# Order of work in a windowed-attention kernel: K's second part in its own bank, odd heads' outer products first, statistics moved behind one transpose

## The chip, the cores and the metric

The kernel runs on one core of one Trainium2 chip. The metric is device time in microseconds (us) for one execution of the whole program.

## What is computed

One block of a conditioned mixer, all in bf16. x has 2048 rows of 512 features. Attention has 32 heads of 16 features and a causal window of 256 rows; a token mixer follows, an MLP over the 2048 rows with 1792 hidden units.

```python
mod = (silu(c) @ w_mod).reshape(1, 6, 1, 512)             # sa, ca, ga, sb, cb, gb
h = layernorm(x) * (1 + ca) + sa
q, k, v = split(h @ wqkv)                                 # 32 heads of 16
p = softmax(where(0 <= i - j < 256, q @ k.T / 4, -1e9))
x = x + ga * ((p @ v) @ wo)
h = layernorm(layernorm(x) * (1 + cb) + sb)
u = gelu(einsum('sd,sf->df', h, w1) + b1)
x = x + gb * (u @ w2 + b2).T
```

## The kernel before

**Stages.** Four groups of rows (tg, 512 rows each) go through attention one after the other. Each has four groups of heads (g8, eight heads each), and each of these has five units k: two units of scores for the even heads (kind A), one for the masked corners of even and odd heads together (kind C, k = 2), and two for the odd heads (kind A). In tg 0 the first two A units are merged for g8 > 0, so that there are 77 units in all. After attention comes the MLP, mostly one long row of matmuls.

**A unit.** `emit_scores` (line 595) lets TensorE write the scores of eight heads into two PSUM tiles `pss` (a ring of three tiles of two banks). `emit_exp` (662) is ScalarE's exponential of each of the two, two a unit. `av_a` (680) multiplies the exponentials of an A unit with V, `av_c` (696) those of the C unit; both add into one PSUM bank, `po`, of which there is only one. I call these the outer products; the even heads' close after k = 2, the odd heads' after k = 4. Then `norm_out` (732) transposes the bank on VectorE (line 735), which frees it, and `norm_rest` (740) divides by the sums (VectorE line 746, GpSimd 747) and transposes back (755). In `av_a` the first matmul of the even or odd heads opens the bank (`start`), and the last of `av_c` closes it (`stop`).

**Other work of the same stretch.** TensorE also computes the projections of Q, K and V, the output projection and the first MLP products, one "group" of 16 matmuls a unit, into the single bank `dn`; VectorE evacuates each (lines 304, 330, 333, 397, 838), and only then can the next group start. VectorE and GpSimd also run the layer norms: `ln1_stats` (225) and `ln1_apply` (250, on GpSimd for tg > 0), `ln23` (758; line 775 is its normalisation) whose results `hb` the groups of `part_group` (822) read.

**The order** is written out by the loop from line 989 on. For each unit it issues the first exponential, the scores of the next unit, outer products that close a bank, the group's matmuls, the second exponential, the group's evacuation, and then the outer products of the unit before. Within that, VectorE's remaining work stands in chains of steps. A planner places them: `clock` holds an estimate of when each engine is free, `fill(until)` (805) issues steps as long as their estimated cost ends before `until` plus a slack (`SLACK`, and `late[0]`), and a step may carry a condition. `products` (960) calls `fill` ahead of each transpose that closes a bank. So a changed cost in the planner moves VectorE's and GpSimd's instructions for the rest of attention.

**The head.** For the first unit Q and K are computed in two parts (`first_qk`, 551): Q's first 320 columns go to a `dn` bank, K's first 128 to a `po` bank, and both second parts to the two banks of one tile, `second` (547), which is one of the three `pss` tiles. VectorE masks Q into even and odd heads (`q_half`, 559), ScalarE copies K (`k_piece`, 567). The first scores need only the first parts; the second unit's scores need the rest, and write the bank pair that `second` held. `modulate` (530) makes the rows that both read, in two column parts, feature blocks 0 and 1 on VectorE, 2 and 3 on ScalarE.

Of the kernel before, what the change touches and what calls it, by code (L numbers as in the profile page):

```python
# [8 lines left out]
DT = mybir.dt  # L9
# [3 lines left out]
P = 128  # L13
S = 2048
D = 512
# [5 lines left out]
ND = D // P  # L21
# [9 lines left out]
def kernel(  # L31
# [67 lines left out]
    part = {fc: ppool.tile([P, D], DT.float32, name=f"part{fc}") for fc in PART}  # L99
# [123 lines left out]
    ln1 = {}  # L223
# [60 lines left out]
    def dense(out, lhsT, rhs, start, stop):  # L284

        for j in range(4):
            cols = slice(32 * j, 32 * j + 32)
            nc.tensor.matmul(  # L288
                out[cols, :], lhsT=lhsT[:, cols], rhs=rhs, start=start, stop=stop,
                tile_position=(0, 32 * j), skip_group_check=True,  # L290
            )
# [123 lines left out]
    with tc.manual_schedule():  # L415
# [130 lines left out]

        second = ps_s.tile([P, 2, 4 * P], DT.float32, name="pss")
        pq2 = (ps_dn.tile([P, 4 * P], DT.float32, name="dn"), second[:, 0, :])
        pk2 = (ps_po.tile([P, 4 * P], DT.float32, name="po"), second[:, 1, :])

        def first_qk(dc, part):
            q_cols, k_cols = ((slice(0, FIRST), slice(0, P)), (slice(FIRST, 4 * P), slice(P, 4 * P)))[part]
            for ps, col0, cols in ((pq2[part], 0, q_cols), (pk2[part], D, k_cols)):
                dense(
                    ps[:, cols], lhsT=wqkv[:, dc, col0 : col0 + P], rhs=h1T[0][:, dc, cols],
                    start=(dc == 0), stop=(dc == ND - 1),
                )

        def q_half(part):
            cols = (slice(0, FIRST), slice(FIRST, 4 * P))[part]  # L560
# [8 lines left out]
            nc.scalar.activation(out=KT[0][0][:, cols], in_=pk2[part][:, cols], func=ACT.Copy)  # L569

        for dc in (0, 2, 1, 3):
            first_qk(dc, 0)
        q_half(0)
        k_piece(0)
        for dc in (0, 2):
            first_qk(dc, 1)

        w1box = {}

# [9 lines left out]
        def a_pieces(tg, i):  # L589
            return [(4 * tg + kb, q0, n, c0) for kb, q0, n, c0 in A_PIECES[i] if 4 * tg + kb >= 0]  # L590
# [71 lines left out]
        def emit_exp(u, a):  # L662
# [14 lines left out]
            )  # L677
            return act.ins

        def av_a(tg, g8, k):  # L680
            kind, par, i = KINDS[k]
            if i == 0:
                state["po"] = ps_po.tile([P, 4 * P], DT.float32, name="po")
            merged = i == 0 and both(tg, g8, 0)
            k, shift = (0, 256 * par) if merged else (k, 0)
            for n, (kb, q0, nq, c0) in enumerate(a_pieces(tg, i)):
                c0 += shift
                for j in range(4):
                    nc.tensor.matmul(  # L689
                        state["po"][32 * j : 32 * j + 32, q0 : q0 + nq],  # L690
                        lhsT=VaugT[kb // 4][:, kb % 4, 8 * g8 + 2 * j + par, :],
                        rhs=state["e", tg, g8, k, j // 2][:, j % 2, c0 : c0 + nq],
                        start=(i == 0 and n == 0), stop=False, tile_position=(0, 32 * j), skip_group_check=True,
                    )

        def av_c(tg, g8, par):
            for b in range(4):
                for half in range(2):
                    if half and 4 * tg + b < 2:
                        continue  # L700
                    c0, q0 = 256 * par + 64 * b, b * P + 64 * half
                    for j in range(4):
                        nc.tensor.matmul(  # L703
                            state["po"][32 * j : 32 * j + 32, q0 : q0 + 64],
                            lhsT=Vc[half][:, b, 8 * g8 + 2 * j + par, :],
                            rhs=state["e", tg, g8, 2, j // 2][:, j % 2, c0 : c0 + 64],
                            start=False, stop=(b, half) == (3, 1), tile_position=(0, 32 * j),
                            skip_group_check=True,
                        )

        def copy_vc(g8, half, b, n, kb):
# [11 lines left out]
        def emit_av(u):  # L723
            tg, g8, k = units[u]
            if k != 2:
                av_a(tg, g8, k)
            if k in (2, 4):
                av_c(tg, g8, k // 4)
                norm_out(k // 4)
                return True  # L730

# [172 lines left out]
        def at_unit(tg, ul, u, behind):  # L904
            if ul == 0 and tg + 1 < NG:
                st = lambda g, t0=0: [
                    (lambda tl=tl: ln1_stats(g, tl), 0.8, lambda tl=tl: 4 * g + tl in loaded) for tl in range(t0, 4)
                ]

                def ap(*tls):  # L910
                    for tl in tls:
                        ln1_apply(tg + 1, tl)
                    return 1.13 * len(tls)
                if tg == 0:
                    steps = st(1, 2)
                    steps[1] = (lambda: (ln1_stats(1, 3), on_pool(ap(2, 3)))[0], *steps[1][1:])
                else:
                    steps = [(lambda tl=tl: ap(tl), 0.0) for tl in range(4)]
                add_chain(steps, first=True)
                if tg == 0:  # L920
                    add_chain(st(2) + st(3))
            if tg == 0 and ul == 8:
                zeros_for(3)
                on_pool(1.9)
            if tg == 0 and ul == 3:
                nc.gpsimd.memset(mod_add[:], 0.0)
                nc.gpsimd.memset(mod_add[32:64, :], 1.0)
                nc.gpsimd.tensor_copy(out=sT_rep[:], in_=sT[:].unsqueeze(2).to_broadcast([P, ND, 32]))
                on_pool(0.9)
            if tg == 0 and 7 <= ul < 11:  # L930
                loaded.update((2 * ul - 6, 2 * ul - 5))
            for n in ((0, 1, 2, 3), (4, 5))[ul] if tg == 0 and ul < 2 else ():
                late_mod(n, behind)
            for g8 in range(ND):
                if ul == ((0, 3, 7, 10) if tg == 0 else (0, 3, 4, 5))[g8] and (g8 or tg < 2):
                    copies_for(tg, g8)
            for n in (6, 7) if tg == 0 and ul == 2 else ():
                late_mod(n, behind)
            if 0 < tg < NG - 1 and ul == 17:
                copies_for(tg + 1, 0)  # L940
            while q_loads and ul != 3:
                load_q(*q_loads.pop(0))
            if tg == 0 and 4 <= ul < 8:
                pair = slice(2 * ul, 2 * ul + 2)
                paced(xall[:, pair, :], x_rows[:, pair, :], behind)
            if tg == 0 and 8 <= ul < 10:
                js = slice(ul % 2 * 2, ul % 2 * 2 + 2)
                paced(wod[:, js, :], wo_v[:, js, :], behind)
            if tg == 1 and ul == 2:
                modw.release()  # L950
                w1box["pool"] = tc.alloc_tile_pool(name="w1pool", bufs=1, side="right")
                w1box["a"] = w1box["pool"].tile([P, NA, F], DT.bfloat16, name="w1a")
                w1box["v"] = B_w1.rearrange("(sc p) f -> p sc f", p=P)
                w1box["sc"] = iter([(sc, n) for sc in range(NA) for n in range(2)])

            for sc, n in [x for x in [next(w1box.get("sc", iter(())), None)] if x]:
                part_f = slice(n * F // 2, (n + 1) * F // 2)
                paced(w1box["a"][:, sc, part_f], w1box["v"][:, sc, part_f], behind)

        def products(u):  # L960
            tg, g8, k = units[u]
            if k in (0, 3):
                clock["pe"] = max(clock["pe"], clock["po"])
            clock["pe"] += (0.34, 0.34, 0.25, 0.34, 0.58)[k]
            if k in (2, 4):
                fill(clock["pe"])
                clock["dve"] = max(clock["dve"], clock["pe"] + 0.05) + 0.73
                clock["po"] = clock["dve"] + 0.1
            if emit_av(u) and k == 4:
                add_chain(norm_rest(tg, g8), first=True)  # L970
# [7 lines left out]
                on_pool(for_pool)  # L978

        emit_scores(0)  # L980
        for dc in (1, 3):
            first_qk(dc, 1)
        q_half(1)
        v0_mms, v0_evac, _ = v_group(0, 0, ps_dn)
        v0_evac(v0_mms())
# [3 lines left out]
        for u, (tg, g8, k) in enumerate(units):  # L989
# [9 lines left out]
            if u + 1 < len(units):  # L999
                emit_scores(u + 1)  # L1000
                if units[u + 1][2] == 2:
                    first = max(clock["pe"], before) + 0.3
                    clock["pe"] = max(first, clock["act"] + 0.05) + 0.42
                else:
                    first = clock["pe"] = max(clock["pe"], clock["act"] - 0.1) + 0.4
                ready[u + 1] = (first + 0.1, clock["pe"] + 0.1)
            for n in range(3) if u == 4 else ():
                products(n)
            closes = u > 0 and units[u - 1][2] in (2, 4) and u != 3
# [9 lines left out]
            group = at.get(ul)  # L1019
            held[0] = u < 4  # L1020

            late[0] = 0.5 if 4 <= u < 8 else 0.0
            if group:
                tile_ = group[0]()
                clock["pe"] = max(clock["pe"], clock["dn"]) + (0.55 if group[2] > 1 else 0.2 if group[2] == 0.2 else 0.9)
# [227 lines left out]
```

## Time and profile before

| what | us |
|---|---|
| median of 3 runs | 258.14 |
| the runs | 257.07 to 258.76 |
| profiled execution | 256.86 |
| its span on the core | 255.2 |
| TensorE, ScalarE, VectorE, GpSimd busy | 237.4, 160.8, 170.2, 132.8 |
| first exponential | 12.41 |
| end of the last exponential | 161.96 |

The profile names engines PE (TensorE matmul), PEld (its weight loads), DVE (VectorE), ACT (ScalarE), POOL (GpSimd) and SP (the queue that issues DMAs). A timeline row gives start, duration, engine, line and operation, output and inputs by the program's names, and in brackets how long the engine had been idle and what is taken to have released it. Consecutive instructions of one kind are merged into one row; since matmuls are pipelined, a row's end lies after the start of the next. The time of an execution is its span and some 1.7 us around it.

### The profile page before, as it was taken

To read this page: it belongs to the slowest core of one execution; us is meant where nothing else is said; L and a number is where in the kernel's file an instruction comes from. 1 tells how busy PE (TensorE), PEld (TensorE's weight loads), DVE (VectorE), ACT (ScalarE), POOL (GpSimd) and SP (SyncE) were. 2 spreads that over 40 slices of the span, in tenths; PEclk is the share of its full clock that TensorE was granted. 3 is DMA by queue.
4 is the path that set the end of the run, shared out by engine and by line. 5 is a ranking of instruction groups with operands and counts; after the bars stand their busy time and mean duration, and the time that the engine had idled before them with its cause. 6 is when DMAs were issued, how large, how long until landed. Compare 5 with 4: busy or idle time off the path is not lost.

```text
span 255.2 us, 11303 instructions
## 1 busy us (share of the span) xinstructions
PE 237.4 (93%) x5011; PEld 127.1 (50%) x5011; DVE 170.2 (67%) x358; ACT 160.8 (63%) x187; POOL 132.8 (52%) x225
## 2 busy tenths in 40 slices
PE   7989879989989999989999999999999999999994
PEld 2534445555555556555555555544444444444443
DVE  5768789795898868988877895689512303342544
ACT  6478999999999999999999999300074220000000
POOL 5696875986368998977726798654200000000000
PEclk9999999999999999999999999999999999999999
DMA  6986715146620714201123200799960000202121
GB/s 174 317 274 198 210 57 157 37 105 145 208 78 21 219 34 85 46 17 24 41 46 68 60 3 6 260 411 410 410 240 0 0 0 3 82 7 75 39 86 41
DMA packets 26260, 29.96 MB, mean 117 GB/s; under 512 B 3940, under 2 KB 22884, under 8 KB 26212
## 3 DMA queue, kind: packets, MB, share of 16 engines
q1 hardware_dynamic: 26212, 29.25, 36.8%
q8 instruction: 39, 0.64, 1.1%
q14 instruction: 9, 0.07, 0.1%
HBM read 22.55 MB, written 2.23 MB: 97 GB/s over the span
## 4 chain that ended last, share of the span: by engine, by line
PE 67%; DVE 24%; DMA 3%; issue 2%; SPq 2%; POOL 1%; ACT 0%; DVEq 0%
PE py L1216 19%; PE dn L288 18%; PE pu L1094 8%; PE pu L1180 6%; DVE t L735 4%; PE pss L608 3%; DVE VaugT L304 3%; PE po L689 3%; PE po L703 3%; DVE KT L330 2%; DVE qs L333 2%; DVE ln_stats L229 2%; DVE x L397 2%; DVE ln_stats L763 1%; PE pa L1116 1%
## 5 line engine op out<-in xcount | busy, mean ns | idle before, releaser
L675 ACT ACTIVATE et<-pss 128x1024 bf16<-128x1024 f32 (+1 forms) x154 | 144.2, 1016 | 4.6 <-PE pss L625 3.2
L1216 PE MATMUL py<-guT,w2r 128*128 128x512 bf16 (+1 forms) x238 | 48.5, 366 | 0.0
L1216 PEld LDWEIGHTS <-w2r 128*128 128x128 bf16 x238 | 23.3, 98 | 25.3
L288 PE MATMUL dn<-h1T,wqkv 128*32 128x512 bf16 (+1 forms) x480 | 31.4, 378 | 3.2 <-DVE qs L333 1.3
L1195 DVE SCALAR_TENSOR_TENSOR o<-py,bFM,bc 128x512 bf16<-128x512 f32 (+1 forms) x17 | 11.7, 716 | 30.5 <-PE py L1216 30.5
L735 DVE STREAM_TRANSPOSE t<-po 128x512 f32<-128x512 f32 x32 | 22.6, 707 | 7.7 <-PE po L703 7.4
L212 POOL TENSOR_TENSOR ln_rstd<-ln_ve,mhalf 128x1 f32<-128x1 f32 (+1 forms) x40 | 24.1, 603 | 3.6 <-DVE ln_ve L208 0.4
L689 PE MATMUL po<-et,VaugT 128*32 128x64 bf16 (+2 forms) x704 | 24.8, 240 | 1.1 <-DVE t L735 1.1
L608 PE MATMUL pss<-QT,KT 32*128 32x64 bf16 (+2 forms) x704 | 24.7, 237 | 0.7 <-ACT KT L569 0.6
L689 PEld LDWEIGHTS <-VaugT 128*32 128x32 bf16 x704 | 18.1, 96 | 12.3 <-issue 4.4
L208 POOL TENSOR_SCALAR ln_ve<-ln_mv 128x1 f32<-128x1 f32 (+1 forms) x39 | 9.1, 234 | 25.1 <-DVE ln_mv L765 13.5
L288 PEld LDWEIGHTS <-wqkv 128*32 128x32 bf16 x544 | 13.7, 95 | 13.0 <-issue 5.5
L608 PEld LDWEIGHTS <-KT 32*128 32x128 bf16 x704 | 13.5, 92 | 13.2 <-issue 4.4
L747 POOL TENSOR_TENSOR merge<-t,zr 128x512 bf16<-128x512 f32 x16 | 16.9, 1058 | 3.6 <-DVE zr L746 3.6
L1105 ACT ACT_TABLE_LOAD x1 | 1.3, 1283 | 24.7 <-DMA w2r<-in_B_w_dram 24.7
L288 PE MATMUL dn<-wqkv,h1T 128*32 128x512 bf16 x224 | 14.7, 380 | 2.2 <-DVE qs L333 0.9
L779 POOL TENSOR_TENSOR h<-h,bc 128x512 bf16<-128x512 bf16 x12 | 13.9, 1160 | 4.7 <-DVE h L775 4.7
L625 PE MATMUL pss<-mask_q,mask_k 32*128 32x256 bf16 (+1 forms) x232 | 16.3, 266 | 0.0
L1103 DVE TENSOR_TENSOR gelu_a<-pu,part 128x512 f32<-128x512 f32 x8 | 5.2, 686 | 16.4 <-PE pu L1180 16.4
L780 POOL TENSOR_TENSOR h<-h,bc 128x512 bf16<-128x512 bf16 x12 | 13.9, 1161 | 0.9
L288 PE MATMUL dn<-wod,OTd 128*32 128x512 bf16 x192 | 12.6, 380 | 1.9 <-DVE part L838 0.7
L1180 PE MATMUL pu<-hb,w1b 128*128 128x512 bf16 x64 | 14.3, 379 | 0.0
(126 smaller groups left out, 377.7 us busy)
## 6 DMA issues: line engine op xcount, KB each, us to landing
w2r<-in_B_w_dram SPq DMA_DIRECT2D x14, 512.0 KB, 10.0
w1a<-in_B_w_dram SPq DMA_DIRECT2D x16, 224.0 KB, 3.7
w1b<-in_B_w_dram SPq DMA_DIRECT2D x8, 448.0 KB, 7.3
wmod<-in_w_mod_dram SPq DMA_DIRECT2D x8, 256.0 KB, 4.3
Vc<-VaugT SPq DMA_DIRECT2D x32, 64.0 KB, 2.8
out_dram<-otile SPq DMA_DIRECT2D x15, 128.0 KB, 1.7
x<-in_A_x_dram SPq DMA_DIRECT2D x7, 256.0 KB, 4.6
Vc<-VaugT SPq DMA_DIRECT2D x12, 128.0 KB, 3.3
```

Source lines behind the costliest of these rows:

```text
L212: nc.gpsimd.tensor_tensor(out=r[:], in0=ve[:], in1=mhalf[:, 0:n], op=ALU.pow)
L288: nc.tensor.matmul(out[cols, :], lhsT=lhsT[:, cols], rhs=rhs, start=start, stop=stop, tile_position=(0, 32 * j), skip_group_check=True,)
L608: nc.tensor.matmul(pss[j // 2][:, j % 2, c0 : c0 + nq], lhsT=keys(kb, g8)[rows[j], k0 : k0 + P], rhs=QT[tg][g8][rows[j], p, q0 : q0 + nq], ...
L625: nc.tensor.matmul(pss[j // 2][:, j % 2, :].rearrange("p (a r) -> p a r", a=2)[:, 0:n, :] .rearrange("p a (b q) -> p a b q", q=64)[:, :, 0 ...
L675: act = nc.scalar.activation(out=et[:, :, 0:n], in_=state.pop((u, a))[:, :, 0:n], func=ACT.Exp, scale=SCORE_SCALE,)
L689: nc.tensor.matmul(state["po"][32 * j : 32 * j + 32, q0 : q0 + nq], lhsT=VaugT[kb // 4][:, kb % 4, 8 * g8 + 2 * j + par, :], rhs=state["e" ...
L735: nc.vector.transpose(out=state["t2"][:, par, :], in_=state["po"][:])
L747: nc.gpsimd.tensor_tensor(out=m[:].rearrange("p (b a d) -> p a b d", a=2, d=DH), in0=t2v[:, :, :, 0:DH], in1=zr[:].to_broadcast([P, 2, 16, ...
L779: nc.gpsimd.tensor_tensor(out=h2[:], in0=h2[:], in1=bc_cb1, op=ALU.mult)
L1094: nc.tensor.matmul(pu[:, i, :], lhsT=w1_of(sc, fc), rhs=hb[sc][:], start=(sc == 0), stop=(sc == NT - 1),)
L1180: nc.tensor.matmul(pu[:, i, :], lhsT=w1_of(sc, fc), rhs=hb[sc][:], start=(sc == s0), stop=(sc == NT - 1),)
L1216: nc.tensor.matmul(pys[n][:, 0 : hi - lo], lhsT=w2r[:, fc, tb * P : (tb + 1) * P], rhs=guT[fc][:, lo:hi], start=(fc == 0), stop=(fc == NF ...
```

## The change

Five edits, with no arithmetic added or left out.

1. Head: K's second part goes to the `po` bank and its first part to the second bank of `second`, beside Q's second part. All of K's second part is computed ahead of the first scores, all of Q's behind them (before, half of each ahead and half behind).
2. For tg > 0 the odd heads' `av_c` opens the bank instead of closing it. It is issued in the iteration of k = 4, right behind the next unit's scores and ahead of that iteration's group; `av_a` of k = 3 then adds, and that of k = 4 closes. The planner's cost of closing the odd heads falls from 0.58 to 0.34, and its slack for tg > 0 rises by 0.12.
3. `av_c` takes its blocks in the order 0, 1, 3, 2.
4. `fill` is not called ahead of the transpose of unit 7, so that no statistics are placed there.
5. A step of `ln1_apply` waits in the planner until its statistics have been placed.

```diff
-        pk2 = (ps_po.tile([P, 4 * P], DT.float32, name="po"), second[:, 1, :])
+        pk2 = (second[:, 1, :], ps_po.tile([P, 4 * P], DT.float32, name="po"))
...
         for dc in (0, 2, 1, 3):
-            first_qk(dc, 0)
+            first_qk("q", dc, 0)
+            first_qk("k", dc, 0)
         q_half(0)
         k_piece(0)
-        for dc in (0, 2):
-            first_qk(dc, 1)
+        for dc in range(ND):
+            first_qk("k", dc, 1)
...
+        def outer_first(tg, par):
+
+            return tg > 0 and par == 1
+
         def av_a(tg, g8, k):
             kind, par, i = KINDS[k]
-            if i == 0:
+            opened = outer_first(tg, par)
+            if i == 0 and not opened:
                 state["po"] = ps_po.tile([P, 4 * P], DT.float32, name="po")
...
-                        start=(i == 0 and n == 0), stop=False, tile_position=(0, 32 * j), skip_group_check=True,
+                        start=(i == 0 and n == 0 and not opened),
+                        stop=(opened and i == 1 and n == len(pieces) - 1),
+                        tile_position=(0, 32 * j), skip_group_check=True,
...
         def av_c(tg, g8, par):
-            for b in range(4):
+            opens = outer_first(tg, par)
+            if opens:
+                state["po"] = ps_po.tile([P, 4 * P], DT.float32, name="po")
+            for b in (0, 1, 3, 2):
...
-                            start=False, stop=(b, half) == (3, 1), tile_position=(0, 32 * j),
-                            skip_group_check=True,
+                            start=(opens and (b, half) == (0, 0)), stop=(not opens and (b, half) == (2, 1)),
+                            tile_position=(0, 32 * j), skip_group_check=True,
...
             if k in (2, 4):
-                av_c(tg, g8, k // 4)
+                if not outer_first(tg, k // 4):
+                    av_c(tg, g8, k // 4)
                 norm_out(k // 4)
...
-                    steps = [(lambda tl=tl: ap(tl), 0.0) for tl in range(4)]
+                    steps = [(lambda tl=tl: ap(tl), 0.0, lambda tl=tl: (tg + 1, tl // 2) in ln1) for tl in range(4)]
...
-            clock["pe"] += (0.34, 0.34, 0.25, 0.34, 0.58)[k]
+            clock["pe"] += (0.34, 0.34, 0.25, 0.34, 0.34 if tg else 0.58)[k]
             if k in (2, 4):
-                fill(clock["pe"])
+                if u != 7:
+                    fill(clock["pe"])
...
         emit_scores(0)
-        for dc in (1, 3):
-            first_qk(dc, 1)
+        for dc in range(ND):
+            first_qk("q", dc, 1)
         q_half(1)
...
+            if k == 4 and outer_first(tg, 1):
+                clock["pe"] = max(clock["pe"], clock["po"]) + 0.25
+                av_c(tg, g8, 1)
             for n in range(3) if u == 4 else ():
                 products(n)
...
-            late[0] = 0.5 if 4 <= u < 8 else 0.0
+            late[0] = 0.5 if 4 <= u < 8 else 0.12 if tg else 0.0
```

More of the change, by code (lines that the diff above doesn't have):

```diff
@@ L548, with first_qk @@
         pq2 = (ps_dn.tile([P, 4 * P], DT.float32, name="dn"), second[:, 0, :])
-        pk2 = (ps_po.tile([P, 4 * P], DT.float32, name="po"), second[:, 1, :])
[L551 to L557, printed above, removed]
+        pk2 = (second[:, 1, :], ps_po.tile([P, 4 * P], DT.float32, name="po"))
+        def first_qk(kind, dc, part):
+            cols = slice(FIRST if kind == "q" else P, 4 * P) if part else slice(0, FIRST if kind == "q" else P)
+            ps, col0 = ((pq2, 0) if kind == "q" else (pk2, D))
+            dense(
+                ps[part][:, cols], lhsT=wqkv[:, dc, col0 : col0 + P], rhs=h1T[0][:, dc, cols],
+                start=(dc == 0), stop=(dc == ND - 1),
+            )
         def q_half(part):
@@ L685, in av_a @@
             k, shift = (0, 256 * par) if merged else (k, 0)
-            for n, (kb, q0, nq, c0) in enumerate(a_pieces(tg, i)):
+            pieces = a_pieces(tg, i)
+            for n, (kb, q0, nq, c0) in enumerate(pieces):
                 c0 += shift
```

## The prediction

> **What bounds the kernel now.** I read the page's busy table and slices first, then ScalarE's timeline, then the timelines of TensorE and VectorE where ScalarE pauses.
>
> ```profile
> PE 237.4 (93%) x5011; PEld 127.1 (50%) x5011; DVE 170.2 (67%) x358; ACT 160.8 (63%) x187; POOL 132.8 (52%) x225
> PE   7989879989989999989999999999999999999994
> ACT  6478999999999999999999999300074220000000
> ```
>
> TensorE looks like the bound everywhere. But in slices 5 to 25 ScalarE is full too: the exponentials of the attention stage. Its timeline shows how full, with every pause in square brackets:
>
> ```profile
> 12.41 0.60 ACT L675 ACTIVATE et<-pss 128x512 bf16<-128x512 f32 x1 [0.43 <-PE pss L625]
> 13.87 0.49 ACT L569 ACTIVATE KT<-pss 128x384 bf16<-128x384 f32 x1 [0.86 <-PE dn L288]
> 14.26 4.47 ACT L675 ACTIVATE et<-pss 128x512 bf16<-128x512 f32 x5
> ...
> 33.48 22.95 ACT L675 ACTIVATE et<-pss 128x1024 bf16<-128x1024 f32 x24 [0.29 <-PE pss L625]
> 56.65 5.96 ACT L675 ACTIVATE et<-pss 128x1024 bf16<-128x1024 f32 x6 [0.21 <-PE pss L625]
> 62.77 52.97 ACT L675 ACTIVATE et<-pss 128x1024 bf16<-128x1024 f32 x56 [0.17 <-PE pss L625]
> ```
>
> 56 exponentials in 52.97 us are 0.946 us each, and from 33.48 to the last end at 161.96 ScalarE pauses six times for 1.08 us in all (0.21, 0.17, 0.18, 0.19, 0.17, 0.16). Between 12.41 and 33.48 it pauses for 2.84 us (0.86, 0.53, 0.33, 0.57, 0.26, 0.29). So attention is bound by ScalarE, and no edit to it can give more than these 3.9 us. After 162 TensorE runs without a gap for 89 us, whatever attention did. The granted clock is 1.00 in every stretch.
>
> **The change part by part.** In the built instruction lists each engine has as many instructions as before; all of it is order and waits.
>
> *Head.* ScalarE's copy of K's second part starts at 13.87. The profile names TensorE as releaser; these rows name another candidate:
>
> ```profile
> 12.80 1.04 PE L288 MATMUL dn<-wqkv,h1T 128*32 128x512 bf16 x16
> 13.37 0.41 DVE L562 TENSOR_SCALAR QT<-pss,mask_odd 128x192 bf16<-128x192 f32 x1
> 13.87 0.49 ACT L569 ACTIVATE KT<-pss 128x384 bf16<-128x384 f32 x1 [0.86 <-PE dn L288]
> 14.41 0.40 PE L608 MATMUL pss<-QT,KT 32*128 32x256 bf16 x12 [0.57 <-ACT KT L569]
> ```
>
> VectorE's second masking of Q ends at 13.78, 0.09 before the copy; V's group ends at 13.84 in a bank that the copy doesn't touch. Q's and K's second parts share one tile, so I take VectorE as the releaser. The Trainium skill (PSUM — Partial Sum Buffer, section PSUM bank collisions raise a hardware error) says that engines on different banks run side by side, which would make this wait the scheduler's and not the chip's; no run here has shown it yet. With K's part in a tile of its own the copy follows the first exponential: 12.41 plus 0.49 (half a full one's 0.946 is 0.47) is 12.9, so K is ready by 13.4 and no longer decides. What is late next: the second scores reuse the shared tile and wait for both Q maskings. K's 16 second matmuls now all run ahead of the first scores: 4 sets of 0.16 (384 of 512 columns; a 512 set takes 0.215 by the group's 0.86 us for four), the last held to about 11.87 by ScalarE's last modulation (four from 9.88, end 11.81). So the first scores, at 12.03, slip by some 0.07. Q's second part then takes 0.37 from 12.37 (sixteen weight loads took 0.37 at 12.30), its last result is there near 12.95, the maskings (0.34 apart, 0.41 long) end near 13.77, and the second scores start near 13.83, not 14.41: **-0.58**. Bounds: 0 if another wait holds the copy, -0.94 if only the copy's start counted (13.87 to 12.93). From there to 19 TensorE's rows stand back to back (14.41, 14.85, 15.83, 16.65, 17.04, 17.91, 18.88), so the gain is carried. Loads: the fourth x tile holds VectorE till 15.06 either way, but the next evacuation that something waits for starts only at 18.14.
>
> *Order of blocks in the outer products (0, 1, 3, 2).* The first unit waits at 23.13 for the copy of block 2; then 8 matmuls follow it and not 16. 32 of them take 0.24 us start to start (131.17 to 131.42), so **-0.06**, between 0 and -0.1.
>
> *No statistics ahead of the transpose of unit 7.*
>
> ```profile
> 31.16 0.68 DVE L229 BATCH_NORM_STATS2 ln_stats<-x 128x6 f32<-128x512 bf16 x1
> 31.88 0.18 DVE L230 BATCH_NORM_AGGREGATE ln_mv<-ln_stats 128x2 f32<-128x6 f32 x1
> 31.97 0.68 DVE L735 STREAM_TRANSPOSE t<-po 128x512 f32<-128x512 f32 x1
> 32.71 0.29 PE L689 MATMUL po<-et,VaugT 128*32 128x256 bf16 x4 [1.15 <-DVE t L735]
> ```
>
> The outer products end at 31.45 (31.09 plus 0.36); without the statistics the transpose starts there, 0.5 sooner, and TensorE's 1.15 us wait halves. ScalarE, next in the chain, had waited 0.29: **-0.29**, between 0 and that. The statistics follow one slot later; their rstd is used by GpSimd tens of us later.
>
> *Odd heads first.* One round of ten exponentials in TensorE's timeline:
>
> ```profile
> 131.17 0.42 PE L703 MATMUL po<-et,Vc 128*32 128x64 bf16 x32
> 131.42 1.05 PE L288 MATMUL dn<-h1T,wqkv 128*32 128x512 bf16 x16
> 132.40 0.41 PE L608 MATMUL pss<-QT,KT 32*128 32x256 bf16 x12
> 133.25 1.05 PE L288 MATMUL dn<-h1T,wqkv 128*32 128x512 bf16 x16 [0.34 <-DVE qs L333]
> ...
> 135.12 0.41 PE L703 MATMUL po<-et,Vc 128*32 128x64 bf16 x32
> 135.35 1.05 PE L288 MATMUL dn<-wod,OTd 128*32 128x512 bf16 x16
> ...
> 140.79 0.42 PE L703 MATMUL po<-et,Vc 128*32 128x64 bf16 x32
> ```
>
> A round takes TensorE 9.62 us (131.17 to 140.79) and ScalarE 9.46: the 0.16 between them is the pause. The odd heads' 32 products (135.12) move to just after the scores of 132.40, into the 0.34 us in which TensorE waits for VectorE's evacuation. 0.24 us leaves the busy part, the round falls to 9.38, and ScalarE has no reason to pause: up to **-1.08**. At the other end this edit loses, below. The even transpose must have emptied the bank: it ends at 132.39 (131.67 plus 0.72) and TensorE arrives at 132.92, 0.53 of room. The group behind the products then waits for VectorE anyhow.
>
> Losses: in the last round no scores stand between, so the products would arrive at 160.82 and the transpose ends at 160.92, **+0.15** with the handover; TensorE works through to the end there, so nothing comes back. And VectorE's and GpSimd's orders change: hb_3, read by the group at 102.60 (its last quarter at 103.25), moves behind one more apply (1.04) and merge (1.06). Adding GpSimd's rows in the new order from the statistics of 85.3 on, I get 103.4 where it was 99.74: 0.15 after it is wanted: **+0.2**, between 0 and +1.2 (one merge row more ahead of it).
>
> Sum: -0.58 - 0.06 - 0.29 - 1.08 + 0.15 + 0.2 = **-1.66 us**. The profiled execution took 256.86 (span 255.2 and 1.7 around it), so 255.2 by its own time; it lies 1.3 under the median of 258.14 (runs 257.07 to 258.76). Carried to that median: **256.5**.
>
> **The rivals.**
>
> *The head's wait is TensorE's, as the profile names it*, and the copy still waits for a matmul group. For it: the name, and 13.84 is nearer to 13.87. Against: another bank. The head then gives nothing: 257.1.
>
> *More pauses go.* The 1.16 us at 20.68, 25.09 and 27.29 shrink as well. Against: there the chain runs through VectorE's evacuations and statistics, which stay. Time 256.5 - 1.2 = 255.3 or less; with the head at its bound (0.36 more) 254.9.
>
> *Slower: the moved products wait for the even transpose.* They stand ahead of a group and of the next scores in TensorE's order, so a late transpose stops all three. It decides once the transpose is over 0.53 late. VectorE does run other work ahead of one: at 97.47 a transpose starts after a reduction rather than at once. If one 0.69 us evacuation stood ahead of it in each of the 12 rounds of the last three groups of rows, each would lose 0.16 (1.9 us) and the 1.08 of pauses would stay: 259.5. If two did (1.38), 0.85 each, 10.2 us: 266.7. Against: in the new VectorE order I find only a 0.41 us normalisation ahead of an even transpose, and that at one place.
>
> *Late statistics*: hb_3 costs its full bound, 1.0 more than taken: 257.5.
>
> *VectorE's rows stretch.* Its normalisations (line 775, 12 of them) last 0.31 to 0.85 us, mean 0.476, and its copies of V (line 306, 8) 0.22 to 0.945, mean 0.460. Over their shortest that is already 2.0 and 1.9 us of stretching beside GpSimd's work. Both engines get new orders; if the stretching doubled and all of it stood ahead of something awaited, it would cost 3.9 us: 260.4, if a quarter did, 257.5. Against: only few of these rows stand ahead of a transpose or an awaited evacuation. The Trainium skill (SBUF — State Buffer, section Who interferes with whom) has a rule for it: VectorE in its two-port modes and GpSimd lock each other out of a shared port pair for a whole instruction. By that rule these rows depend on who issues first, which a new order changes; the spread of the rows above agrees.
>
> **How the numbers follow.** Forecast 0.55; head without gain 0.12; more pauses gone 0.18; slower by the even transpose 0.06; late statistics 0.05; stretched rows 0.04, half of it past 1%. About 1% is what a measurement of this kernel can tell from no change (2.6 us; the three runs alone span 1.7). Only "more pauses" passes 1% downward, with a little of the forecast's own spread: faster 0.21, within 1% 0.71, slower 0.08. The range goes from 254.6 (more pauses gone, bounds met) to 258.2 (late statistics with half a us of spread between runs); the slower rival and the far end of the stretched rows lie outside.
>
> **What would show it.** Head: the copy of K's second part starts at 12.9 to 13.0, before the maskings end, and the second scores at 13.8; at 13.8 and 14.4 the step is wrong. Unit 7: transpose at once after the products, TensorE's 1.15 us wait at most 0.7. Odd heads: in each round the 32 products directly behind the scores, the group behind them without a wait over 0.1 us, ScalarE without pauses from 33 to 160. hb_3: a GpSimd wait on the group's last quarter near 102. I am wrong if ScalarE's pauses stay near 1 us or new ones stand behind the moved products.

## The result: 0.5% slower

The changed kernel took a median of 258.85 us (257.96 to 260.27), the kernel before 257.59 (256.47 to 258.76), 14 runs each. The ratio is 1.0049, with a 95% interval of 1.0026 to 1.0072: 1.3 us slower, where 1.7 faster was forecast, and above the forecast's range. The profiled execution took 259.11, its span 257.2 (before 255.2).

The page after, busy time by engine:

```profile
PE 239.2 (93%) x5011; PEld 127.3 (49%) x5011; DVE 171.3 (67%) x358; ACT 159.3 (62%) x187; POOL 132.6 (52%) x225
```

Nothing stands out here: no engine is busier by more than 1.8 us, and the granted clock is 1.00. What is new is where GpSimd waits. These are its waits for VectorE's normalisations from 33 us to its last merge, before and after (us in total, times, the longest):

```profile
POOL h L779 <- DVE h L775: 4.7, 6, 2.2
POOL h L792 <- DVE h L788: 8.7, 9, 2.1
```

With the same work, GpSimd waits longer inside attention, and so it is still at work when its last merge could start.

All of the head lies 0.3 later in this execution (first matmul of Q at 10.56 and not 10.26), ahead of anything that was changed; I take that off where times are compared. ScalarE's timeline after:

```profile
13.31 0.48 ACT L569 ACTIVATE KT<-po 128x384 bf16<-128x384 f32 x1
...
19.57 1.09 ACT L676 ACTIVATE et<-pss 128x512 bf16<-128x512 f32 x2 [1.02 <-PE pss L626]
...
52.51 15.00 ACT L676 ACTIVATE et<-pss 128x1024 bf16<-128x1024 f32 x16 [0.34 <-PE pss L626]
68.22 20.43 ACT L676 ACTIVATE et<-pss 128x1024 bf16<-128x1024 f32 x22 [0.71 <-PE pss L626]
89.45 3.92 ACT L676 ACTIVATE et<-pss 128x1024 bf16<-128x1024 f32 x4 [0.79 <-PE pss L656]
93.88 37.71 ACT L676 ACTIVATE et<-pss 128x1024 bf16<-128x1024 f32 x40 [0.52 <-PE pss L626]
132.01 29.76 ACT L676 ACTIVATE et<-pss 128x1024 bf16<-128x1024 f32 x32 [0.42 <-PE pss L626]
```

The small pauses of 0.16 to 0.21, one in some of the rounds, are gone, as forecast. But five others have come, 2.78 us in all, and the head's pause at 19 grew from 0.53 to 1.02. Two of the five, 0.71 and 0.79, stand behind stops of TensorE that no engine released (in a view, *issue* means that the profile shows nothing that was waited for):

```profile
66.39 0.21 PE L715 MATMUL po<-et,Vc 128*32 128x64 bf16 x3 [0.73 <-issue]
...
88.01 0.83 PE L288 MATMUL dn<-wqkv,h1T 128*32 128x512 bf16 x11 [0.63 <-issue]
```

The last exponential ends at 161.77 (before 161.96): 0.5 sooner by the shifted clock. Yet the span is 2.0 longer, so most of the loss lies behind attention. There TensorE stops in the first output projection of the last rows:

```profile
167.90 1.25 PE L1133 MATMUL pa<-wod,OTd 128*128 128x512 bf16 x5 [1.73 <-DVE OTd L768]
```

It waits for the last `OTd`, that for the last merge, and the merge stands in GpSimd's queue. GpSimd's timeline after:

```profile
164.93 1.15 POOL L793 TENSOR_TENSOR h<-h,bc 128x512 bf16<-128x512 bf16 x1
166.04 1.06 POOL L760 TENSOR_TENSOR merge<-t,zr 128x512 bf16<-128x512 f32 x1
```

and before:

```profile
163.91 1.06 POOL L747 TENSOR_TENSOR merge<-t,zr 128x512 bf16<-128x512 f32 x1 [2.03 <-DVE zr L746]
```

The order of these last rows is the same in both. Before, GpSimd had been idle for 2.03 us when the last merge's operand came; after, that operand was ready at 164.12 (the reciprocal, 163.77 plus 0.35) and the merge went 1.9 later, because GpSimd was still busy with the layer norms of earlier tiles. 0.30 of start, -0.12 at the end of TensorE's attention work (162.76 against 162.58) and 1.73 of this wait make 1.9 of the 2.0.

### The profile page after: what moved, and what is told of

Its sections match the earlier page's. It is cut to its first block, busy times and chain, and to the rows that moved or that the text cites. A ratio compares the mean times of both kernels' runs of the same rounds, so it can differ in the third digit from the quotient of the medians.

```text
span 257.2 us, 11303 instructions
## 1 busy us (share of the span) xinstructions
PE 239.2 (93%) x5011; PEld 127.3 (49%) x5011; DVE 171.3 (67%) x358; ACT 159.3 (62%) x187; POOL 132.6 (52%) x225
## 4 chain that ended last, share of the span: by engine, by line
PE 62%; DVE 19%; POOL 12%; issue 3%; DMA 2%; SPq 1%; POOLq 0%
PE py L1233 19%; PE dn L288 14%; PE pu L1111 7%; PE pu L1197 6%; PE pss L609 4%; DVE t L748 3%; PE po L715 3%; PE po L696 3%; DVE VaugT L304 3%; POOL ln_rstd L212 2%; DMA wmod<-in_w_mod_dram 2%; POOL h L793 2%; POOL h L792 2%; DVE ln_stats L776 2%; POOL merge L760 2%
## 5 line engine op out<-in xcount | busy, mean ns | idle before, releaser
L676 ACT ACTIVATE et<-pss 128x1024 bf16<-128x1024 f32 (+1 forms) x154 | 142.7, 1025 | 6.5 <-PE pss L626 4.9
L609 PE MATMUL pss<-QT,KT 32*128 32x64 bf16 (+2 forms) x704 | 25.4, 237 | 0.0
L208 POOL TENSOR_SCALAR ln_ve<-ln_mv 128x1 f32<-128x1 f32 (+1 forms) x39 | 9.2, 235 | 24.6 <-DVE ln_mv L778 12.9
L1120 DVE TENSOR_TENSOR gelu_a<-pu,part 128x512 f32<-128x512 f32 x8 | 5.2, 686 | 16.4 <-PE pu L1197 16.4
L288 PE MATMUL dn<-hb,w1a 128*32 128x512 bf16 x208 | 13.8, 380 | 0.9 <-DVE part L851 0.7
```

What stands on the lines that cost most here:

```text
L288: nc.tensor.matmul(out[cols, :], lhsT=lhsT[:, cols], rhs=rhs, start=start, stop=stop, tile_position=(0, 32 * j), skip_group_check=True,)
L609: nc.tensor.matmul(pss[j // 2][:, j % 2, c0 : c0 + nq], lhsT=keys(kb, g8)[rows[j], k0 : k0 + P], rhs=QT[tg][g8][rows[j], p, q0 : q0 + nq], ...
L676: act = nc.scalar.activation(out=et[:, :, 0:n], in_=state.pop((u, a))[:, :, 0:n], func=ACT.Exp, scale=SCORE_SCALE,)
```

## The experiments

Ratios are to the kernel before, with 95% intervals. Each kernel ran beside the kernel before, whose median was between 257.12 and 258.20 there, so kernels of different series are compared by their ratios. Theory 1: the planner's new numbers, which reorder VectorE and GpSimd, lose the time, and the matmuls' new order gains what was forecast. Theory 2: the moved products lose it.

### TensorE's new order with VectorE's and GpSimd's old order

```diff
-                    steps = [(lambda tl=tl: ap(tl), 0.0, lambda tl=tl: (tg + 1, tl // 2) in ln1) for tl in range(4)]
+                    steps = [(lambda tl=tl: ap(tl), 0.0) for tl in range(4)]
...
-            clock["pe"] += (0.34, 0.34, 0.25, 0.34, 0.34 if tg else 0.58)[k]
+            clock["pe"] += (0.34, 0.34, 0.25, 0.34, 0.58)[k]
...
-                if u != 7:
-                    fill(clock["pe"])
+                fill(clock["pe"])
...
             if k == 4 and outer_first(tg, 1):
-                clock["pe"] = max(clock["pe"], clock["po"]) + 0.25
                 av_c(tg, g8, 1)
...
-            late[0] = 0.5 if 4 <= u < 8 else 0.12 if tg else 0.0
+            late[0] = 0.5 if 4 <= u < 8 else 0.0
```

> TensorE's order as in the changed kernel (head, block order, odd heads first), VectorE's and GpSimd's order exactly as before: none of the planner's changes (costs, slack, unit 7, condition). Theory 1, the loss comes from the new VectorE and GpSimd order, which leaves GpSimd's last merge behind a layer norm: here the last merge starts near 164 as before, TensorE has no wait near 165, and the time is 0.5 to 1.5 us under before. Theory 2, the moved products themselves lose the time (they wait for the bank, and TensorE's order is worse): the time stays 1 us or more over before.

Measured: 256.31 us, ratio 0.9952 (0.9929 to 0.9975), 1.2 us faster. ScalarE's timeline of this kernel:

```profile
56.52 103.48 ACT L676 ACTIVATE et<-pss 128x1024 bf16<-128x1024 f32 x110 [0.19 <-PE pss L626]
```

110 exponentials without a pause that the view shows: the odd heads' edit does what it was forecast to do. GpSimd's last merge waits for its operand again, and not in a queue:

```profile
162.12 1.05 POOL L760 TENSOR_TENSOR merge<-t,zr 128x512 bf16<-128x512 f32 x1 [1.95 <-DVE zr L759]
```

### The planner's numbers alone

TensorE's order is that of before; cost, clock, slack, unit 7 and condition are changed as in the diff.

> TensorE's order as before, VectorE's and GpSimd's order as in the changed kernel: only the planner's numbers are changed. Theory 1: TensorE waits 1.5 to 2 us near 165 for the last merge, and the time is 1.3 to 2 us over before. Theory 2: within 0.4 us of before.

Measured: 259.67, ratio 1.0097 (1.0064 to 1.0129), 2.5 us slower, more than the 1.3 to 2 expected. The last merge starts at 166.29, and TensorE waits for it:

```profile
168.15 1.25 PE L1119 MATMUL pa<-wod,OTd 128*128 128x512 bf16 x5 [1.62 <-DVE OTd L755]
```

The two halves add up: -0.48% and +0.97% make the +0.49% of the whole change. Theory 2 is out.

### The last merge ahead of one tile's layer norm

```diff
-            return [(p1, 0.8), (p2, 0.37, lambda: len(live) < LIVE), (p3, 0.8)]
+            return [(p1, 0.8), (p2, 0.37, lambda: len(live) < LIVE and (tb != 11 or "closed" in state)), (p3, 0.8)]
...
         add_chain(norm_rest(NG - 1, ND - 1), first=True)
+        state["closed"] = True
```

> The changed kernel, but the normalisation of the last tile of rows of the earlier groups (tile 11) is placed behind the last merge, so GpSimd's last merge no longer stands behind its two row operations (2.3 us). Theory 1: the merge starts near 164.1 and not 166.04, TensorE's 1.73 us wait near 166 goes, and the time falls by 1.5 to 1.9 us against the changed kernel, to 0.3 to 0.6 under before. Theory 2: as the changed kernel, 1.3 over before.

Measured: 258.12, ratio 1.0017 (0.9995 to 1.0039): 0.7 less than the changed kernel, less than half of what was expected. The merge starts at 163.71, and the wait of 1.73 is gone. But the delayed layer norm now stands in VectorE's queue ahead of the projection's evacuations, and TensorE waits there instead:

```profile
168.67 1.02 PE L1134 MATMUL pa<-wod,OTd 128*128 128x512 bf16 x4 [0.56 <-DVE x L1138]
```

This 0.56 and one of 0.50 at 170.19 came for 1.73, which leaves 0.67, near the 0.7 that was measured. It is not the whole account, since the two profiled executions differ inside attention too. Here TensorE stops for only 0.17 with nothing that it waits for, near 66, and comes to the group that reads `hb_3` sooner, at 101.79 and not 103.32. It then waits longer for the group's last quarter, 1.02 us where the changed kernel's waits 0.19, and ScalarE pauses 0.92 behind it:

```profile
103.64 0.40 PE L288 MATMUL dn<-hb,w1a 128*32 128x512 bf16 x4 [1.02 <-POOL hb L219]
```

Late work that is moved aside is still late.

### Which of the planner's numbers

First the changed kernel with unit 7's call of `fill` restored:

> The changed kernel with unit 7 as before: of the planner's changes the cost 0.34, the clock and the slack stay, and VectorE's order is that of the changed kernel but for 5 places. If the cost and the slack are what lets statistics in ahead of V's evacuations and puts GpSimd's work late, it is as slow as the changed kernel within 0.5 us (1 to 1.8 over before), with the last merge near 166. If it is unit 7's left-out call that shifts everything behind it, the last merge starts near 164 and the time is under before.

Measured: 259.31, ratio 1.0069 (1.0048 to 1.0091), the last merge at 165.53 with GpSimd busy ahead of it. TensorE waits 1.00 for `hb_3` here as well. Unit 7 is not it; cost, clock, slack and the condition of edit 5 are left. They can't be taken apart completely: with the lower cost and no slack the planner does not get a layer norm done before the group that reads it. The slack alone, on the old order:

> The run with the old order, plus the planner's slack of 0.12 alone (costs, clock and unit 7 as before). VectorE's order towards the end of attention is then that of before, so if the lower cost of the closing and the clock beside it are what put GpSimd's last layer norms late, the last merge starts at its usual place without a queue, and the time is that of the old order, 256.0 to 256.8. If the slack does it, the last merge stands in the queue and the time is 258 to 259.5.

Measured: 259.02, ratio 1.0033 (1.0003 to 1.0062), 0.8% over the run without the slack. Each branch of the expectation is half right: the last merge stands in no queue (GpSimd had been idle for 1.96), as in the first, but the time is that of the second, lost inside attention. TensorE's waits from 33 to 158, by what released it, in the run with the old order:

```profile
PE dn L288 <- DVE VaugT L304: 0.8, 4, 0.2
```

with the slack alone:

```profile
PE dn L288 <- DVE VaugT L304: 2.9, 6, 0.8
```

(us in total, times, the longest.) In the changed kernel it is 2.3 in five, in the kernel before 0.9 in four. VectorE's timeline of the changed kernel shows one such place:

```profile
127.83 0.93 DVE L306 COPY Vc<-VaugT 64x256 bf16<-64x256 bf16 x1
128.68 0.68 DVE L776 BATCH_NORM_STATS2 ln_stats<-x 128x6 f32<-128x512 bf16 x1
...
129.49 0.66 DVE L304 CAST VaugT<-dn 128x512 bf16<-128x512 f32 x1
```

and that of before:

```profile
128.79 0.69 DVE L304 CAST VaugT<-dn 128x512 bf16<-128x512 f32 x1 [0.47 <-PE dn L288]
```

Statistics (0.68, and 0.18 for their aggregation) stand between a copy of V that lasts 0.93 and the next evacuation of V, which starts 2.32 behind the one before it (127.17) and not 1.77 as in the kernel before (127.02); the next group waits 0.65 for it (at 130.20), and ScalarE's pause of 0.42 follows at 132.01. In the kernel before VectorE was idle there for 0.47, waiting for TensorE. The pause at 93.88 has the same place and cause. The one at 52.51 does not: there statistics stand ahead of V's second evacuation in the kernel before too (at 51.22). So I left the slack out in the first two units of each later group of rows, in which V is evacuated (the "group of heads" of the expectation means these):

```diff
-            late[0] = 0.5 if 4 <= u < 8 else 0.12 if tg else 0.0
+            late[0] = 0.5 if 4 <= u < 8 else 0.12 if tg and ul > 1 else 0.0
```

> The changed kernel with the slack of 0.12 left out in the two units of each group of heads' start where V is evacuated (ul 0 and 1). If the slack lets statistics in ahead of V's second evacuation there, ScalarE's pauses of 0.3 to 0.5 near 52, 93 and 132 go, and the time falls by 0.5 to 1.2 against the changed kernel; the last merge stays late. If the pauses stay, another of the planner's numbers places the statistics.

Measured: 258.56, ratio 1.0011 (0.9988 to 1.0033). By the ratios that is 0.4% under the changed kernel, within what was expected, though the two intervals just overlap. The reason isn't the expected one: pauses of 0.26, 0.51 and 0.72 stand at 54, 93 and 131, TensorE still waits 2.4 us for `VaugT`, and statistics stand there as before (127.96 to 128.80). The planner's lower cost, its new clock, or the slack left in the other units places them. That statistics stand ahead of V's evacuations is shown; which number puts them there in the changed kernel is not.

### The head alone

Only edit 1, on the kernel before.

> Only the head's edit, all else as before. By the prediction's step: 0.58 us under before. By the rows of the changed kernel, where K is ready 0.86 sooner but TensorE is held at 16.4 to 17.0 with nothing that it waits for, and the gain is gone behind that: 0 to 0.3 under. If the hold-up is not in this run, the gain is seen in the time.

Measured: 257.16, ratio 1.0002 (0.9982 to 1.0021): nothing; the forecast's 0.58 would be 0.9977, just outside the interval. The step works: in the changed kernel the copy of K goes at 13.31, while VectorE masks Q until 14.09. But TensorE's timeline after has this:

```profile
14.02 0.63 PE L609 MATMUL pss<-QT,KT 32*128 32x256 bf16 x10
...
16.96 0.24 PE L646 MATMUL pss<-QT,KT 32*64 32x128 bf16 x2 [0.59 <-issue]
```

and before this:

```profile
16.65 0.24 PE L645 MATMUL pss<-QT,KT 32*64 32x128 bf16 x2 [0.19 <-issue]
```

The second scores start 0.69 sooner than before (14.02 against 14.41 plus 0.3), V's group 0.38 sooner (14.77 against 14.85 plus 0.3), and the last two score matmuls of unit 2 not at all (16.96 against 16.65 plus 0.3). Before, these two stood 0.19 idle, after 0.59, with the head alone 0.82, and nothing that the profile shows released them.

### What holds TensorE at 16.4 to 17.0

The page lists a queue that brings instructions:

```profile
q8 instruction: 39, 0.64, 1.0%
```

39 packets and 0.64 MB are 16 KB each. TensorE has 5011 matmuls and 5011 weight loads. If all the packets are TensorE's, one holds about 257 instructions, some 128 matmuls with their weight loads. By the trace's DMA records the packet of this stretch ran from 14.42 to 15.52. If TensorE is held for its next instructions, the place follows from counting. The idle matmuls that run while the first x is loaded make that easy to try, by splitting eight of them into nine narrower ones each (64 more):

```diff
-        def warm(n):
+        def warm(n, parts=1):
             for i in range(n):
-                nc.tensor.matmul(idle, lhsT=identity[:], rhs=zero[:, 0 : 4 * P], start=True, stop=True)
+                for m in range(parts):
+                    cols = slice(4 * P * m // parts, 4 * P * (m + 1) // parts)
+                    nc.tensor.matmul(idle[:, cols], lhsT=identity[:], rhs=zero[:, cols], start=True, stop=True)
...
-        warm(3)
+        warm(1)
+        warm(2, 9)
...
-        warm(6)
+        warm(6, 9)
```

> As the run with the old order, but eight of the ten idle matmuls that run before the first x is there are split into nine narrower ones each: 64 more TensorE matmuls and weight loads, the same columns. Theory, the stall near 16.4 to 17.0 is the arrival of the next 256 TensorE instructions (128 matmuls and their weight loads, 16 KB), and its place is fixed by counting instructions: the stall at the 223rd matmul moves 64 matmuls up, to a place where TensorE waits anyway, the scores of unit 2 run through, and the 0.5 us of the head come out at last: 0.4 to 0.6 under the old order's time, ScalarE's pause of 0.98 near 19.3 falls to 0.4 to 0.5. Rival, the stall belongs to that instruction or to the x tiles that arrive then: it stays where it is, and the time is that of the old order.

Measured: 255.00, ratio 0.9902 (0.9875 to 0.9930), 0.5% under the old order. The stall in the head is gone, and ScalarE's pause near 19 fell from 0.98 to 0.44. In the profiled execution, with 256.55 the slowest of six, TensorE is held elsewhere instead: 0.53 at 60.54, 0.22 at 69.37 and 0.16 at 90.72. Then 128 more in place of 64, which must bring it back:

> As the run with the old order, with 128 more idle matmuls (eight of the ten split into 17 each) instead of 64. If instruction arrivals stand at every 128th matmul, 128 more of them bring the arrival back to where it was: TensorE held again ahead of the last two matmuls of unit 2's scores near 16.4 to 17, ScalarE's pause near 19.3 back at 0.9 to 1.1, and the time back at the old order's 256.3. If splitting idle matmuls helps by itself, the stall stays away and the time is 255.0 as with 64.

Measured: 256.09, ratio 0.9947 (0.9926 to 0.9968), the old order's time, and the stall is back ahead of the same two matmuls:

```profile
16.76 0.24 PE L649 MATMUL pss<-QT,KT 32*64 32x128 bf16 x2 [0.34 <-issue]
```

ScalarE's pause near 19.4 was 0.77, a little under the expected 0.9. So the place goes by the count, with a period of 128 matmuls, and not by the instruction or by splitting. With 80 more:

> As the best version, with 80 more idle matmuls instead of 64. If instruction arrivals hold TensorE at places fixed by counting matmuls, every 128th, the stall that stood in front of a group's sixth matmul at 68.5 to 69.4 comes 16 matmuls sooner, ahead of that group or not at all, and the head stays free of one: time 254 to 255.2. If they are not fixed by the count, stalls stand at the same places as with 64.

Measured: 255.75, ratio 0.9927 (0.9892 to 0.9961). The place is as expected by the count: the head has no stall, and the one that stood in front of the group's sixth matmul with 64 more (0.77 at 68.54 in the best version, below) stands 16 matmuls sooner, ahead of the group (0.63 at 69.25). But the time is over the expected 254 to 255.2, and in the profiled execution, with 257.82 the slowest of eleven, TensorE is also held 1.26 at 90.86. The control, 64 more on the kernel before:

> The kernel before, with only the eight idle matmuls split as in the fetch run: 64 more TensorE matmuls ahead of the head. It is the control for that step. In the kernel before TensorE was held only 0.19 us at 16.65, so if the gain of the split is that stall alone, 0.2 us or less under before; if the split gives more than the stall that the profile shows (a warmer start, or stalls elsewhere in runs that were not profiled), up to 1 us under before.

Measured: 257.01, ratio 0.9962 (0.9933 to 0.9990). The best estimate, 1.0 us, is more than the 0.19 stall of the first profile; the interval reaches down to 0.3. So the split gives about as much without the head's edit, and how much of its 0.5% is the head's gain come out at last is not shown. In the profiled execution the head's stall is gone, and TensorE is held 0.48 at 60.95 and 0.72 at 91.67. The kernel before once more:

> The kernel before once more, to see in a second execution whether TensorE is held at instruction arrivals behind the head (at matmul 222 plus a multiple of 128), which its first profile did not show. If such stalls of 0.3 to 1 us differ from one execution to the next, they appear here near 66 or 88 as in the changed kernel, and they are no part of what the change does. If they belong to the changed order, there are none here.

Measured: 256.91 in one run, TensorE held 0.34 at 16.93, so the head's stall is in the kernel before as well and differs between executions. Of the stalls near 66 and 88 there is none. One or both are in most of the kernels with the odd heads first, though not in the run with the old order, and the kernel before has two like them with 64 more matmuls. So they can't be put down to the changed order. What the traces show beside the count is that the packets of stalls come late: over the eight executions in which every matmul was recorded, the packets of the 17 stalls in head and attention began 28 to 83 matmuls behind the previous such place (median 64), the others at a median of 23. Why a packet begins late stays open.

### Unit 7 alone, and the best version

On the old order, unit 7's transpose issued ahead of its statistics, the planner's clocks untouched:

```diff
+            if u == 7:
+                emit_av(u)
             if k in (2, 4):
                 fill(clock["pe"])
...
-            if emit_av(u) and k == 4:
+            if u != 7 and emit_av(u) and k == 4:
```

> As the run with the old order, with unit 7's transpose ahead of its statistics and nothing else moved. By the prediction's step TensorE's wait of 1.15 us near 32.7 falls to 0.7 or less and ScalarE's pause of 0.29 at 33.5 goes. Rival: the statistics behind it delay the next evacuation, and the pause stays within 0.1.

Measured: 256.44 in one run. TensorE's wait is 0.73 and ScalarE's pause of 0.29 is gone, as in the changed kernel; the time, by this one run, is not under the old order's 256.31:

```profile
32.55 0.29 PE L696 MATMUL po<-et,VaugT 128*32 128x256 bf16 x4 [0.73 <-DVE t L748]
```

With the 64 idle matmuls as well:

> The run with the split idle matmuls, and unit 7's transpose issued ahead of its statistics, without the planner's clocks being changed (VectorE's order is that of before but for this one swap). If both steps give what they should: 0.5 from the instruction arrival and 0.3 from unit 7 under the old order's 256.31, so 255.5, that is 0.8% under before. If unit 7's wait is replaced by another: 255.8.

Measured: 254.95, ratio 0.9886 (0.9858 to 0.9913): 2.4 us under the kernel it was run beside (257.39), and faster than both kernels. It is more than the 0.8% expected. Unit 7's part of it is not separated by the times (0.9886 against 0.9902).

## Why the prediction was wrong, point by point

TensorE's new order (head, block order, odd heads) was forecast at -1.57 with the loss in the last round, and gave -1.2. The planner's numbers were forecast at -0.29 for unit 7 and +0.2 for the new orders, and gave +2.5. So nearly all of the miss is in the second part.

- **Odd heads first, -1.08: right.** In each round the products stand directly behind the scores; TensorE's timeline after:

```profile
142.42 0.41 PE L609 MATMUL pss<-QT,KT 32*128 32x256 bf16 x12
...
142.87 0.42 PE L715 MATMUL po<-et,Vc 128*32 128x64 bf16 x32
143.28 1.05 PE L288 MATMUL dn<-wod,OTd 128*32 128x512 bf16 x16
```

With the old order of VectorE ScalarE doesn't pause from 56.5 to the end. The group behind the products starts 0.41 after them where 32 products take 0.24, so some 0.17 of its wait is left, a little over the 0.1 of the sign. From 33.5 to the last exponential's end that kernel took 126.5 us where before took 128.5, but only 0.84 of this is idle time; ScalarE's busy time fell as well, from 126.5 to 125.4, with the same 134 exponentials. The prediction had no such term (its ceiling counted pauses alone), and why they follow each other closer is not shown. In times, TensorE's new order gave 1.2 us in all. The even transposes were never late, and the rival by them didn't come. The +0.15 of the last round is not seen: the products at 161.09 stand there without a wait.
- **"And VectorE's and GpSimd's orders change: hb_3 ... +0.2": this step failed.** I followed the new order to one reader, `hb_3`, and searched VectorE's order for work ahead of even transposes. I followed neither the evacuations, where statistics moved in ahead of V's (0.52 and 0.42 of ScalarE's pauses), nor GpSimd's queue to its end, where the last merge was behind (1.73). The sentence "After 162 TensorE runs without a gap for 89 us, whatever attention did" failed with it: it stopped at 166. Alone these orders cost 2.5 us. The 2.03 us for which GpSimd was idle ahead of the last merge were the cover, and they stood in the profile of before. Even the price of `hb_3` came out by luck. The group's last quarter waits 0.19 for it at 104.34 in the changed kernel, but TensorE had been held up at 66.39 and 88.01 there; in the run with the merge first and the one with unit 7 restored, where it was held less, it waits 1.02 and 1.00, which is near the step's far bound of 1.2 and is the rival "late statistics". The sum took TensorE's arrival from before, 103.25, and not the sooner one that its own gains would bring: with the last merge moved, TensorE is there at 102.62 (103.64 less 1.02).
- **Head, -0.58: right as a mechanism, no gain.** The copy of K no longer waits: it runs beside the masking, at 13.31 (forecast 12.9 to 13.0, plus 0.3 of start), and the second scores come 0.69 sooner. That VectorE was the releaser before fits this, but the edit also moved K's matmuls ahead, so it isn't shown by itself. ScalarE reads the `po` bank from 13.31 to 13.79 while TensorE fills `dn` from 13.05 on, which agrees with what the Trainium skill (PSUM — Partial Sum Buffer, section PSUM bank collisions raise a hardware error) says of different banks. "TensorE's rows stand back to back ..., so the gain is carried" failed: one of these rows, 16.65, had 0.19 of idle time put down to issue, and by the runs with added matmuls it is the arrival of instructions, which doesn't come sooner when the work does.
- **Block order, -0.06: consistent.** The pause at 25.1 is 0.50 and not 0.57; with the head alone it is 0.56.
- **Unit 7, -0.29: right in the trace** (1.15 to 0.73, where 0.7 at most was forecast, and the pause gone); that it shows in the time is not shown. The same edit moves later steps in the planner, and the experiment without it shows that these moves were not what cost.
- **VectorE's rows stretch:** the copies of V in this stretch (line 306, six of them) last 0.561 on the mean after, 0.411 before, up to 1.03 where they share the time with GpSimd's operations. That agrees with the rule that the prediction cites from the Trainium skill (SBUF — State Buffer, section Who interferes with whom). But it is 0.9 us in all, and with the old order, which lost nothing, the mean is 0.533. The normalisations did not stretch (0.477 on the mean, before 0.476), so this rival didn't come.

## What to carry to other kernels

When a change moves a planner's costs, compare the orders it makes for every engine, and follow each queue to its last reader, above all where attention hands over to the next stage; an idle gap ahead of a last operation is the slack that the new order will eat. Keep the matmuls' order and the planner's numbers as two changes: here one gained 1.2 us, and the other lost 2.5. And a row whose idle time is put down to issue can be a bound of its own: in this head, work that came sooner only waited there longer.

## What the runs showed of the hardware

TensorE's instructions arrive in packets of 16 KB, about 128 matmuls and their weight loads, and where a packet comes late TensorE is held for it. In 16 profiled executions I count 32 stalls over 0.15 us put down to issue (leaving out one of 0.16 at the start of the MLP that many have), and 29 of them stand ahead of a matmul whose number, counted from 0, is 222 plus a multiple of 128 (a missing record allowed for). All 29 are in the head and attention. They last 0.16 to 1.26 us and end 1.1 to 1.6 us after their packet's end; a packet takes from 0.88 to 2.24 us, the longest ahead of the stall at 88.01. Splitting idle matmuls so that there were 64 more took 0.5% off the run with the old order, and 128 more took nothing off.
